# Retention attention into an MLP on one core: y of chunks 2 to 5 for four batches in one block instead of two pairs

## The chip, the cores and the metric

One core of a Trainium2 chip runs the whole kernel. The time is that of the device for one execution, in microseconds; of several runs the median is given. All operands of the matrix products are 16-bit floats (f16), accumulated in 32 bits (f32).

## The reference

Four batches, eight heads, 768 time steps, head size 64. A recurrence with a decay per head gives y, which then goes through an MLP with a tanh-approximated GELU.

```
gamma = 1.0 - 2.0 ** (-5.0 - np.arange(H))
for t in range(S):
    state = gamma * state + einsum('bhd,bhe->bhde', k[:, :, t], v[:, :, t])
    y[:, :, t] = scale * einsum('bhd,bhde->bhe', q[:, :, t], state)
x = y.transpose(0, 2, 1, 3).reshape(B * S, H * D)      # 3072 x 512
h = x @ w_in                                           # 512 -> 2048
out = gelu_tanh(h) @ w_out                             # 2048 -> 512
```

## The kernel before, in words

**Chunks.** Time is cut into six chunks of 128 steps (c = 0 to 5). Within a chunk and a batch b the recurrence becomes matrix products. A = k·q of the chunk (`mm_A`, L272), masked to the causal part on VectorE (`ev_A`, L285, which writes `a_sb`); y = state·q (`mm_yc`, L294) plus v·A (`mm_yi`, L307), accumulated in one PSUM bank and copied to `xT` (`ev_Y`, L231 on ScalarE, L233 on VectorE); S = k·v (`mm_s`, L326), added on VectorE to the decayed state (`ev_S`, L343); the decay for the next chunk on GpSimd (`decay`, L352). A batch takes 8 small matmuls for A (two heads at a time, on the two halves of the array's rows), 4 for `mm_yc` (the whole array), 8 for `mm_yi` (the two halves of its columns), 4 for S (the whole array).

**q and k.** They arrive by DMA from SyncE's queue (`load`), are scaled to f16 on GpSimd (`prep`: L206 for q and kT, L195 for k, L192 for v; for q and kT of chunks 3 to 5, and q of chunk 2), and are transposed per batch by `att_T`: on VectorE (L258), and for k of chunk 2 on TensorE (`mm_T`, L249) with a copy out of PSUM on VectorE (L233). `mm_A` reads the result, `qkT`.

**MLP.** `moe1` (L419) makes 128 hidden features of a chunk for all four batches with 4 matmuls, and ScalarE does the GELU (L434); `moe2` (L452) multiplies back, batch by batch, 16 matmuls each, and `ev_O` copies out (L474 on ScalarE, L472 on VectorE for batch 3) and issues the store from GpSimd's queue (L479).

**Order.** There is no planner for the schedule: instructions go to each engine in the order in which the program emits them. `run(units, after)` emits a list of MLP units, and behind unit i whatever `after[i]` lists. For the loop at L664 the units of chunk c are 16 of `moe1` (0 to 15), then four of `moe2` for each of the four batches (16 to 31), 4 matmuls each; between them the attention of chunk n = c+1 is woven. Chunk 2 (n = 2) is woven into the two runs at L633 and L651: 16 units of `moe1_two` of chunk 1 (8 matmuls of 256 columns each), then 16 units of `moe2` of chunk 1. Each engine is in order, so an instruction that waits holds those behind it.

**`att_AY`** (L369) takes a list of batches `bs` whose y is made and a list `abs_` whose A is made. It emits `mm_yc` of `bs`, `mm_A` of `abs_`, `mm_yi` of `bs`, then the evictions. In chunks 3 to 5 it is called behind unit 12 (A of batches 0 and 1), 18 (y of 0, 1 and A of 2, 3) and 25 (y of 2, 3).

**PSUM.** Eight banks: "h" 2, "o" 2, "att" 4, each handed out in rotation. A of two batches takes all four att banks (`mm_A` takes two for a batch, one for each half of the rows); S and the transposes on TensorE take one att bank each. y of a pair took the two h banks, which `moe1` uses before and after.

Of the kernel before, what the change touches and what calls it, by code (L numbers as in the profile page):

```python
# [16 lines left out]
def kernel(  # L17
# [10 lines left out]
    B, H, S, Dh = q.shape  # L28
# [29 lines left out]
    att = ctx.enter_context(tc.tile_pool(name="att", bufs=4))  # L58
# [170 lines left out]
    def copy_on(eng, out, in_):  # L229
        if eng is nc.scalar:  # L230
            eng.copy(out=out, in_=in_)  # L231
        else:
            eng.tensor_copy(out=out, in_=in_)  # L233
# [5 lines left out]
    def bank(tag, dt=F32, shape=(128, NHP, 128), name="ps"):  # L239
        return psum.tile(list(shape), dt, tag=tag, bufs=BANKS[tag], name=name)  # L240
# [26 lines left out]
    def mm_A(c, b):  # L267
        t = qkT[c, b]
        ps = [bank("att", name=f"a_ps{j}") for j in range(2)]
        for hp in range(NHP):  # L270
            for j in range(2):
                nc.tensor.matmul(  # L272
                    out=ps[j][:, hp],
                    lhsT=t[j * 64:(j + 1) * 64, 1, hp],
                    rhs=t[j * 64:(j + 1) * 64, 0, hp],
                    start=True,
                    stop=True,
                )
        pss["A", c, b] = ps

    def ev_A(c, b):
        ps = pss.pop(("A", c, b))
        for j in range(2):
            s = att.tile([128, NHP, 128], F16, tag=f"a{j}", name=f"a_sb{j}")
            nc.vector.tensor_tensor(out=s, in0=ps[j], in1=mask[:, j], op=ALU.mult)  # L285
            a_sb[c, b, j] = s

    def mm_yc(c, b, tag):
        y_ps = pss["Y", c, b] = bank(tag, name="y_ps")
        if c == 0:  # L290
            return

        for hp in range(NHP):
            nc.tensor.matmul(  # L294
                out=y_ps[:, hp],
                lhsT=st[:, hp, b],
                rhs=qkT[c, b][:, 0, hp],
                start=(hp == 0),
                stop=False,
                skip_group_check=True,  # L300
            )

    def mm_yi(c, b):
        y_ps = pss["Y", c, b]
        for hp in range(NHP):
            for j in range(2):
                nc.tensor.matmul(  # L307
                    out=y_ps[j * 64:(j + 1) * 64, hp],
                    lhsT=h16["v", c, b][:, 2 * hp + j],
                    rhs=a_sb[c, b, j][:, hp],  # L310
                    start=(c == 0),
                    stop=True,
                    skip_group_check=True,
                )

    def ev_Y(c, b, eng=nc.vector):
        if c not in xT:
            xT[c] = xp.tile([128, NHP, B * C], F16, tag="x", name="xT")
        copy_on(eng, xT[c][:, :, b * C:(b + 1) * C], pss.pop(("Y", c, b)))
# [30 lines left out]
    def decay(c, b):  # L350
        if c + 2 < NCk:
            nc.gpsimd.tensor_tensor(  # L352
                out=stg[:, :, b],
                in0=st[:, :, b],
                in1=cst[:, OG:OG + NHP].unsqueeze(2).broadcast_to([128, NHP, 128]),
                op=ALU.mult,
            )
# [6 lines left out]
    def att_S(c, b, tag="att"):  # L364
        mm_s(c, b, tag)
        ev_S(c, b)
        decay(c, b)

    def att_AY(c, bs, tag, ca, abs_, eng):  # L369


        for b in bs:
            mm_yc(c, b, tag)
        for b in abs_:
            mm_A(ca, b)
        for b in bs:
            mm_yi(c, b)
        if tag == "o":
            for b in abs_:
                ev_A(ca, b)  # L380
        for b in bs:
            ev_Y(c, b, eng)
        if tag != "o":
            for b in abs_:
                ev_A(ca, b)
# [50 lines left out]
    def moe1(c, fc):  # L436
        h_ps = bank("h", shape=(128, B * C), name="h_ps")
        moe1_mm(c, fc, h_ps, 0, B * C)
        gelu(g_tile(c, fc)[:, fc % 2], h_ps)
# [57 lines left out]
    def run(units, after):  # L497
        for i, u in enumerate(units):
            u()
            for f, *args in after.get(i, ()):  # L500
                f(*args)

    VE, AC, PO, SY = nc.vector, nc.scalar, nc.gpsimd, nc.sync
# [85 lines left out]
    def units2(c, b, n=4, tag="o"):  # L589
        u = [(lambda i=i: moe2(c, b, range(i, i + n), tag)) for i in range(0, NF, n)]  # L590
        last = u[-1]
        u[-1] = lambda: (last(), ev_O(c, b))
        return u
# [9 lines left out]
    for b in range(B - 1):  # L603
# [8 lines left out]
            8: [(preps, 1, 0)],  # L612
            10: [(att_T, 1, 0), (preps, 1, 1)],
            11: [(att_AY, 1, (), "att", 1, (0,), None)],
            12: [(att_T, 1, 1), (preps, 1, 2)],
            13: [(att_AY, 1, (0,), "h", 1, (1,), AC)],
            14: [(att_T, 1, 2), (preps, 1, 3), (att_S, 1, 0)],
            15: [(att_AY, 1, (1,), "h", 1, (2,), AC), (att_T, 1, 3), (att_S, 1, 1)],
        },
    )  # L620
# [9 lines left out]
    for nm in "kqv":  # L630
        for b in range(B):
# [11 lines left out]
            6: [(att_S, 1, 3)],  # L643
            8: [(att_T, 2, 0), (load, 3)],
            10: [(att_T, 2, 1)],
            12: [(att_AY, 1, (), "o", 2, (0, 1), None)],
            14: [(att_T, 2, 2)],
            15: [(att_T, 2, 3)],
        },
    )  # L650
    run(  # L651
        [x for b in range(B) for x in units2(1, b)],
        {
            2: [(att_AY, 2, (0, 1), "h", 2, (2, 3), AC)],
            4: [(att_S, 2, 0)],
            5: [(att_S, 2, 1)],
            8: [(att_AY, 2, (2, 3), "h", 2, (), AC)],
            10: [(att_S, 2, 2)],
            11: [(att_S, 2, 3)],
        },  # L660
    )

# [1 line left out]
    for c in range(2, NCk - 1):  # L664
        n = c + 1
        after = {
            2: [(prep, n, 0)],
            4: [(prep, n, 1)],
            6: [(prep, n, 2), (att_T, n, 0)],
            8: [(prep, n, 3), (att_T, n, 1)],  # L670
            9: [(load, n + 1)] if n + 1 < NCk else [],
            12: [(att_AY, n, (), "att", n, (0, 1), None)],
            13: [(att_T, n, 2)],
            15: [(att_T, n, 3)],
            18: [(att_AY, n, (0, 1), "h", n, (2, 3), VE)],
            20: [(att_S, n, 0)],
            21: [(att_S, n, 1)],
            25: [(att_AY, n, (2, 3), "h", n, (), AC)],
            27: [(att_S, n, 2)],
            28: [(att_S, n, 3)],  # L680
        }
        run(
            [(lambda fc=fc: moe1(c, fc)) for fc in range(NF)]
            + [x for b in range(B) for x in units2(c, b)],
            after,
        )
    c = NCk - 1
# [36 lines left out]
```

## Time and profile before

| | |
|---|---|
| median of 5 runs | 215.22 us (215.04 to 216.4) |
| profiled execution | 216.08 us, of which the span of the core is 214.3 us |
| TensorE (PE) busy | 206.8 us, 96% of the span, at full granted clock |
| VectorE (DVE), ScalarE (ACT), GpSimd (POOL) busy | 85.7, 86.6, 96.9 us |
| MLP matmuls of 512 columns | 16 units of 4 in a chunk; L452 88.1 us and L419 86.3 us busy in all |
| A, mask on DVE (L285) | 48 instructions, 682 ns each |
| chunk 2's attention ends and chunk 2's MLP begins | 87.14 us |
| MLP of chunks 3, 4, 5 begins | 119.28, 151.43, 182.51 us |

The engines' names in the profile are those in brackets; PEld is TensorE's weight load. In the chain of work each line has a start, a duration from one start to the next, and the engine with the tensor that it writes. In the timeline each line has a start, the busy time, the engine and line of the program, the operation, and in square brackets the idle time before it with what ended it. Matmuls overlap in the pipe, so a single matmul's duration (379 ns for 512 columns) is longer than its spacing (216 ns); the chain gives spacings.

### The profile page before, as it was taken

The page shows a single profiled execution, that of the slowest core. Times are in us where ns is not written, and L with a number is a line of the kernel's source. Part 1 is how long each engine was busy: PE and PEld are TensorE (multiplying, and loading weights), DVE is VectorE, ACT ScalarE, POOL GpSimd, SP SyncE. Part 2 cuts the span into 40 slices and gives each one's busy share as a digit, 9 for nine tenths or more (in the row PEclk, how much of TensorE's full clock was granted, in tenths as well). Part 3 has the DMA queues.
Part 4 walks back from the last instruction along what each step waited for, and adds up shares of the span by engine and source line. Part 5 has one row for each costly group of instructions (what it writes and reads, how often), then busy time and mean ns, then how long its engine had stood idle before and what let it go on. Part 6 is the DMA issues. An engine that isn't in the chain of part 4 may idle for free.

```text
span 214.3 us, 3906 instructions
## 1 busy us (share of the span) xinstructions
PE 206.8 (96%) x1535; PEld 111.9 (52%) x1535; DVE 85.7 (40%) x156; ACT 86.6 (40%) x149; POOL 96.9 (45%) x117
## 2 busy tenths in 40 slices
PE   7899999999998999999999999999999999999992
PEld 2468444467896554444545444545444554444461
DVE  5468000299529443235673335673335640100000
ACT  2467670335464313465113465113465113565110
POOL 2898100253828463699353799221599221100000
PEclk9999999999999999999999999999999999999999
DMA  6999999999879788998878987889900012100121
GB/s 154 288 238 206 206 202 227 235 245 200 164 185 234 111 164 161 238 256 135 126 150 185 284 179 114 125 164 246 284 11 3 0 70 80 49 0 0 52 98 50
DMA packets 124802, 32.79 MB, mean 153 GB/s; under 512 B 118064, under 2 KB 122928, under 8 KB 124784
## 3 DMA queue, kind: packets, MB, share of 16 engines
q1 hardware_dynamic: 106800, 20.22, 48.3%
q0 software_dynamic: 6112, 8.65, 17.3%
q10 hardware_dynamic: 11872, 3.67, 7.3%
q8 instruction: 12, 0.20, 0.4%
q14 instruction: 6, 0.05, 0.1%
HBM read 30.44 MB, written 6.29 MB: 171 GB/s over the span
## 4 chain that ended last, share of the span: by engine, by line
PE 75%; DMA 16%; POOL 4%; DVE 2%; SPq 1%; issue 0%; ACT 0%; DVEq 0%
PE o_ps L452 34%; PE h_ps L419 31%; DMA w_out<-in_moe_w_out_dram 9%; DMA k<-in_k_dram 3%; PE y_ps L307 3%; DMA q<-in_q_dram 3%; PE a_ps L272 3%; PE y_ps L294 2%; PE s_ps L326 2%; DMA out_dram<-o_sb 2%; POOL w_in L400 1%; PE qkT_ps L249 1%; POOL k L195 1%; DVE qkT L258 1%; POOL w_out L409 1%; SPq L98 0%
## 5 line engine op out<-in xcount | busy, mean ns | idle before, releaser
L452 PE MATMUL o_ps<-w_out,g 128*128 128x512 f16 (+1 forms) x400 | 88.1, 371 | 0.0
L419 PE MATMUL h_ps<-xT,w_in 128*128 128x512 f16 (+2 forms) x480 | 86.3, 337 | 0.0
L434 ACT ACTIVATE g<-h_ps 128x512 f16<-128x512 f32 (+1 forms) x98 | 57.7, 589 | 49.3 <-PE h_ps L419 49.1
L419 PEld LDWEIGHTS <-w_in 128*128 128x128 f16 x480 | 44.6, 98 | 37.1
L452 PEld LDWEIGHTS <-g 128*128 128x128 f16 x400 | 37.6, 98 | 38.9
L285 DVE TENSOR_TENSOR a_sb<-a_ps,mask 128x512 f16<-128x512 f32 x48 | 30.1, 682 | 16.2 <-PE a_ps L272 16.1
L195 POOL TENSOR_TENSOR k<-k,cst 128x512 f16<-128x512 f32 x24 | 25.3, 1063 | 11.0 <-DMA k<-in_k_dram 11.0
L479 POOL DMA_DIRECT2D out_dram<-o_sb x17 | 9.6, 568 | 45.2 <-ACT o_sb L474 35.6
L474 ACT COPY o_sb<-o_ps 128x512 f32<-128x512 f32 x19 | 11.0, 586 | 40.9 <-PE o_ps L452 37.8
L352 POOL TENSOR_TENSOR stg<-st,cst 128x512 f32<-128x512 f16 x16 | 16.6, 1046 | 10.8 <-DVE st L343 9.9
L343 DVE TENSOR_TENSOR st<-s_ps,stg 64x256 f16<-64x256 f32 x32 | 13.5, 421 | 17.8 <-PE s_ps L326 17.2
L206 POOL TENSOR_TENSOR q<-q,cst 128x512 f16<-128x512 f32 x16 | 16.6, 1046 | 4.7 <-DMA out_dram<-o_sb 4.6
L258 DVE STREAM_TRANSPOSE qkT<-q 128x512 f16<-128x512 f16 x16 | 11.2, 699 | 15.7 <-POOL q L206 15.7
L195 DVE TENSOR_TENSOR q<-q,cst 128x512 f16<-128x512 f32 x8 | 6.7, 836 | 23.0 <-DMA q<-in_q_dram 22.9
L231 ACT CAST xT<-y_ps 128x512 f16<-128x512 f32 x15 | 8.3, 588 | 11.2 <-PE y_ps L307 11.2
L206 POOL TENSOR_TENSOR kT<-kT,cst 128x512 f16<-128x512 f32 x12 | 12.5, 1044 | 0.0
L171 PE MATMUL spin_ps<-zero 128*128 128x512 f16 x31 | 10.2, 479 | 1.3 <-DVE zero L139 1.3
L491 DVE COPY o_sb<-o_ps 128x256 f32<-128x256 f32 x1 | 0.4, 425 | 25.2 <-PE o_ps L452 25.2
L192 POOL CAST v<-v 128x512 f16<-128x512 f32 x16 | 9.7, 606 | 0.8 <-DMA v<-in_v_dram 0.8
L272 PE MATMUL a_ps<-qkT 64*128 64x128 f16 x192 | 8.3, 218 | 1.5 <-DVE qkT L233 0.8
L190 ACT CAST v<-v 128x512 f16<-128x512 f32 x7 | 4.3, 621 | 12.2 <-DMA k<-in_k_dram 8.7
L258 DVE STREAM_TRANSPOSE qkT<-kT 128x512 f16<-128x512 f16 x12 | 8.3, 691 | 1.8 <-POOL kT L206 1.8
(36 smaller groups left out, 95.7 us busy)
## 6 DMA issues: line engine op xcount, KB each, us to landing
v<-in_v_dram SPq DMA_DIRECT2D x20, 256.0 KB, 4.6
k<-in_k_dram SPq DMA_DIRECT2D x19, 256.0 KB, 5.0
out_dram<-o_sb POOLq DMA_DIRECT2D x17, 256.0 KB, 3.4
q<-in_q_dram SPq DMA_DIRECT2D x64, 64.0 KB, 2.8
kT<-in_k_dram SPq DMA_DIRECT2D x48, 64.0 KB, 3.1
w_out<-in_moe_w_out_dram POOLq DMA_DIRECT2D x4, 512.0 KB, 17.8
q<-in_q_dram SPq DMA_DIRECT2D x6, 256.0 KB, 6.0
w_in<-in_moe_w_in_dram POOLq DMA_DIRECT2D x3, 512.0 KB, 11.6
```

Source lines behind the costliest of these rows:

```text
L171: nc.tensor.matmul(out=ps, lhsT=zero[:, 0:128], rhs=zero, start=True, stop=True)
L195: eng.tensor_tensor(out=t, in0=src, in1=cst[:, col:col + H].unsqueeze(2).broadcast_to([128, H, Dh]), op=ALU.mult,)
L206: nc.gpsimd.tensor_tensor(out=t, in0=ld_all((key, c))[:, b * NHP:(b + 1) * NHP].rearrange("p hp a d -> p (hp a) d"), in1=cst[:, col:col + ...
L258: nc.vector.transpose(out=t[:, i].rearrange("p hp t -> p (hp t)"), in_=blk16.pop((nm, c, b)).rearrange("p ha d -> p (ha d)"),)
L272: nc.tensor.matmul(out=ps[j][:, hp], lhsT=t[j * 64:(j + 1) * 64, 1, hp], rhs=t[j * 64:(j + 1) * 64, 0, hp], start=True, stop=True,)
L285: nc.vector.tensor_tensor(out=s, in0=ps[j], in1=mask[:, j], op=ALU.mult)
L343: eng.tensor_tensor(out=st[sl, :, b, sl], in0=s_ps[sl, :, sl], in1=stg[sl, :, b, sl], op=ALU.add,)
L352: nc.gpsimd.tensor_tensor(out=stg[:, :, b], in0=st[:, :, b], in1=cst[:, OG:OG + NHP].unsqueeze(2).broadcast_to([128, NHP, 128]), op=ALU.mult,)
L419: nc.tensor.matmul(out=out, lhsT=w_in_sb[wi][:, kc, wr * 128:(wr + 1) * 128], rhs=xT[c][:, kc, t0:t1], start=(kc == 0), stop=(kc == NHP - ...
L434: nc.scalar.activation(out=out, in_=in_, func=AF.Gelu_apprx_tanh, scale=1.0)
L452: nc.tensor.matmul(out=ps[:, n0:n1], lhsT=g_sb[c, fc // 2][:, fc % 2, b * C:(b + 1) * C], rhs=w_out_sb[fc // (NF // NO)][:, fc % (NF // NO ...
L474: nc.scalar.copy(out=o_sb, in_=ps)
```

## The change

A new function `att_Y` makes y of all four batches together: `mm_yc` of the four, into the two h banks (batches 0, 1) and two att banks (2, 3), then `mm_yi` of the four, then the evictions, in turn on ScalarE and VectorE. The pairs of A are made by calls of `att_AY` without y. In chunk 2 A of batches 0 and 1 moves from behind unit 12 to behind unit 13 of `moe1_two`, with the transposes of batch 2 directly behind it; A of batches 2, 3 stands behind unit 1 of `moe2`, y behind unit 4 and the four S behind 6 to 9. In chunks 3 to 5 `att_T` of batch 2 stands before A of batches 0, 1, that of batch 3 one unit earlier, A of batches 2, 3 behind unit 17, y behind unit 21 and the four S behind 23 to 26.

```diff
+    def att_Y(c):
+
+        tags = ("h", "h", "att", "att")
+        for b in range(B):
+            mm_yc(c, b, tags[b])
+        for b in range(B):
+            mm_yi(c, b)
+        for b in range(B):
+            ev_Y(c, b, (AC, VE)[b % 2])
...
             10: [(att_T, 2, 1)],
-            12: [(att_AY, 1, (), "o", 2, (0, 1), None)],
-            14: [(att_T, 2, 2)],
+            13: [(att_AY, 2, (), "att", 2, (0, 1), None), (att_T, 2, 2)],
             15: [(att_T, 2, 3)],
...
-            2: [(att_AY, 2, (0, 1), "h", 2, (2, 3), AC)],
-            4: [(att_S, 2, 0)],
-            5: [(att_S, 2, 1)],
-            8: [(att_AY, 2, (2, 3), "h", 2, (), AC)],
-            10: [(att_S, 2, 2)],
-            11: [(att_S, 2, 3)],
+            1: [(att_AY, 2, (), "att", 2, (2, 3), None)],
+            4: [(att_Y, 2)],
+            6: [(att_S, 2, 0)],
+            7: [(att_S, 2, 1)],
+            8: [(att_S, 2, 2)],
+            9: [(att_S, 2, 3)],
...
+            10: [(att_T, n, 2)],
             12: [(att_AY, n, (), "att", n, (0, 1), None)],
-            13: [(att_T, n, 2)],
-            15: [(att_T, n, 3)],
-            18: [(att_AY, n, (0, 1), "h", n, (2, 3), VE)],
-            20: [(att_S, n, 0)],
-            21: [(att_S, n, 1)],
-            25: [(att_AY, n, (2, 3), "h", n, (), AC)],
-            27: [(att_S, n, 2)],
-            28: [(att_S, n, 3)],
+            14: [(att_T, n, 3)],
+            17: [(att_AY, n, (), "att", n, (2, 3), None)],
+            21: [(att_Y, n)],
+            23: [(att_S, n, 0)],
+            24: [(att_S, n, 1)],
+            25: [(att_S, n, 2)],
+            26: [(att_S, n, 3)],
```

## Prediction

> **What bounds the kernel now.** I read the page's chain that ended last first. TensorE carries it, with the MLP's two matmul lines on top:
>
> ```profile
> PE 75%; DMA 16%; POOL 4%; DVE 2%; SPq 1%; issue 0%; ACT 0%; DVEq 0%
> ```
>
> The DMA share lies in the start, before 41 us, which the change doesn't touch. From there to the end TensorE is the path, so the change is worth what it does to TensorE's own stream: its busy time, and its waits. Next the waits of TensorE, and of its weight loads, from 60 to 190 us. In this stretch there are only two places, the second seen at the weight loads:
>
> ```profile
> PE a_ps L272 <- DVE qkT L233: 0.8, 2, 0.5
> ```
> ```profile
> PEld L326 <- DVE a_sb L285: 1.0, 2, 0.5
> ```
>
> The chain in order of time shows what they cost. Chunk 2 first, where A is woven into the first MLP half of chunk 1:
>
> ```profile
> 62.83 1.06 POOL q L206
> 63.89 0.02 issue
> 63.91 0.72 DVE qkT L258
> 64.64 0.02 issue
> 64.66 0.42 DVE qkT L233
> 65.08 0.56 DVE qkT L258
> 65.64 0.38 DVE qkT L233
> 66.02 0.05 issue
> 66.07 0.40 PE a_ps L272 x8
> 66.47 1.85 PE h_ps L419 x16
> ```
>
> For a stretch TensorE isn't the path here: q of chunk 2 lands, GpSimd scales it at 62.83, VectorE transposes two batches one after the other, and A of batch 1 starts at 66.07. The timeline says when TensorE was ready: its 16 matmuls of units 11 and 12 start at 62.96 and take 1.74, so it was free at 64.70. A of two batches takes 0.55 where nothing waits (below), so 66.47 - 64.70 - 0.55 = 1.2 us are lost.
>
> Then chunk 3, the same view; chunks 4 and 5 have the same numbers within 0.02:
>
> ```profile
> 98.36 0.55 PE a_ps L272 x16
> 98.91 2.70 PE h_ps L419 x12
> 101.61 2.59 PE o_ps L452 x12
> 104.20 0.45 PE y_ps L294 x8
> 104.65 0.55 PE a_ps L272 x16
> 105.20 0.57 PE y_ps L307 x16
> 105.77 1.83 PE o_ps L452 x8
> 107.60 0.00 issue
> 107.60 0.40 PE s_ps L326 x4
> ```
>
> Two things. S takes 0.40 where it takes 0.22 everywhere else: 0.18 of waiting for the first att bank that the mask of A (L285) gives back. And each change between whole-array and half-array matmuls costs: twelve MLP matmuls take 2.59, but 2.70 behind A; eight take 1.73 (2 x 0.863), but 1.83 behind y. L307 takes 0.34 for 8 (chunk 1, at 56.77) and 0.57 for 16, so 0.11 of a block is fixed and each further batch costs 0.23; A is the same (0.33, 0.55). L294 has no such part (0.22, 0.45).
>
> **The change part by part.** *Matmuls.* None is added or removed: A, y and S have the same counts. What changes is the number of passages between array shapes. Before, per chunk: into A, out; into A (behind L294), from A into L307, out; into L307, out: seven, 0.11 each. After: into A, out, into A, out, into L307, out: six. Worked out: two A 1.10, out of each 0.22, L294 for four 0.90, L307 for four 0.57 + 2 x 0.23 = 1.03, out 0.10: 3.35. Before: 0.55 + 0.11 + 0.45 + 0.55 + 0.57 + 0.10 + 0.45 + 0.57 + 0.10 = 3.45. A gain of 0.10 to 0.11 in each of four chunks: 0.44. The Trainium skill (TensorEngine Tiling, Key Properties) says that changing the tiling mode drains the engine; the rows price it. By rule and rows the gain is 0.44; if the fixed part belonged to the pair of batches, it would be nothing.
>
> *The wait of S, chunks 3 and 4.* S now stands two units (1.73 us) behind y; its att banks are those of A of batch 3, masked long before, and those of y of batches 2 and 3, copied out in 0.6 us on each of two engines. Gone: 2 x 0.18 = 0.36. What is late next there is nothing: the h banks of y are needed again only by the next chunk's first unit, eight units later.
>
> *Chunk 2, first half.* A moves behind unit 13. TensorE does that unit from 64.70 to 65.57 in the time that it now waits. A of batch 0 runs at 65.57 (its qkT is there at 65.08), A of batch 1 still at 66.07, to 66.40. Then the added wait: the transposes of batch 2 stand directly behind, and need an att bank, all four of which A holds. The mask of the first starts 0.4 us behind A (98.36 to 98.72 in chunk 3), at 65.98, takes 0.68, and the release reaches TensorE 0.06 later (107.54 to 107.60 at S): 66.72, a wait of 0.3. Queued behind it are units 14 and 15 and all of `moe2`; ScalarE's GELU waits for those, with nothing late. Then 0.22 + 1.74 + 0.22: `moe2` starts at 68.90, against 69.64 in the chain. Gain 0.74. Bounds: if the unprofiled runs get q 0.8 earlier, the old wait was only 0.4 and the new bank wait eats the gain (-0.1); without the bank wait it would be 1.1.
>
> *Chunk 2, second half.* VectorE's four masks and two transposes with copies take 4.31 from their start (65.93 to 70.24 before); from 65.98 qkT of batch 3 is ready at 70.29. A of batches 2, 3 stands at 68.90 + 1.73 = 70.63: no wait, by 0.3 and 0.3 more for batch 3. Masks end at 73.5; y starts at 73.9 and needs the last mask 1.5 later. The four S cost 0.22 each as before. Only the 0.11 changes: chunk 2's MLP starts at 69.64 - 0.74 + 17.50 - 0.11 = 86.29, against 87.14.
>
> *Chunk 3, the transposes.* Batch 2's go ahead of the masks of A(0, 1) on VectorE and wait there for GpSimd. GpSimd doesn't move with TensorE: k of batch 0 lands at 91.2 and it works without a gap from there (the profile's only wait is there).
>
> ```profile
> 97.36 1.05 POOL L206 TENSOR_TENSOR kT<-kT,cst 128x512 f16<-128x512 f32 x1
> ...
> 100.93 1.05 POOL L206 TENSOR_TENSOR kT<-kT,cst 128x512 f16<-128x512 f32 x1
> ```
>
> So VectorE transposes kT of batch 2 at 98.44, the masks run from 99.05 to 101.5 (before 98.72), kT of batch 3 from 102.05 to 102.76. TensorE, 0.85 earlier than before, does A(0, 1) at 97.51, then 0.55 + 0.11 + 2.59 + 1.73: A of batch 2 at 102.49, of batch 3 at 102.82. It just fits: the cover is zero, and any further delay of GpSimd is paid one to one. I take 0 (bounds -0.3 to 0.6). In chunks 4 and 5 GpSimd begins behind the store of batch 3's output and so moves with TensorE: in the clock of before kT of batch 3 is transposed at 134.4, and A(3) would stand at 130.51 + 0.66 + 2.59 + 1.73 + 0.33 = 135.8; 1.4 to spare. The stores on GpSimd's queue keep their order against the preps; the loads on SP keep theirs, and none waits for a moved instruction.
>
> *Evictions.* y goes half to ScalarE, half to VectorE in every chunk. They have 0.6 us spacing, and the next reader of `xT` is ten units off. The same page's section PSUM Bottleneck speaks against the change here: packing speeds up TensorE but not the emptying of PSUM, and two more banks are held. By the rows the emptying is 4 x 0.6 over two engines, 1.2 us, against 1.73 until S wants a bank: nothing; without that cover the third S would wait.
>
> **Sum.** 0.74 + 4 x 0.11 + 2 x 0.18 = 1.54. The profiled execution is 216.08 with a span of 214.3: it gives 214.54 and a span of 212.8. The median is 215.22, 0.86 below the profiled one; by the same step 213.7.
>
> **The rivals.**
> *Little is left (215.22 to 214.2).* The 1.2 us of chunk 2 hang on when q lands. If it lands earlier in unprofiled runs, or if chunk 3 takes the gain back because GpSimd's k lands when it lands and A(3) waits, the 0.74 goes: 215.22 - 0.80 = 214.4. For it: the cover of 0 in chunk 3 and the 0.86 between profile and median. Against it: the chain shows the DMA far ahead of chunk 2 and the loads' order on SP unchanged.
> *Slower.* VectorE is in order, and the transposes of batch 2 now stand in front of the masks of A(0, 1). If GpSimd is late by L, VectorE stands, the att banks stay taken, and A(2, 3), one unit and a y block earlier than before, stops TensorE in chunks 3, 4 and 5. Price: L in chunk 3, L - 1.4 in each of the others. From L = 1.45 it eats the 1.54, from 1.8 the kernel is slower by over 0.5%; at L = 2: 2 + 2 x 0.6 - 1.54 = 1.7 more, 216.9. For it: GpSimd has no pause from 91 to 103 and no slack in chunk 3. Against it: it keeps the same queue, and in chunks 4 and 5 waited for no load.
>
> **Chances.** The forecast 58%, little left 27%, slower 10%, better than forecast (no bank wait, 213.2 or below) 5%. Within 0.5% (1.08 us, about what a measurement of this kernel can tell from no change) is from 214.1 to 216.3; a small part of the second case lies below that. Faster 0.63, same 0.27, slower 0.10. Range 213.0 to 215.1: it takes in the second case, and leaves out the slower one and half of the better.
>
> **What would show it.** In the chain after: `moe2` of chunk 1 starting near 68.9, with a wait of L249 for L285 of some 0.3 and none of note at A; L307 x32 at 1.03; S at 0.22 everywhere; MLP of chunk 3 starting near 118.1. I am wrong if A in chunk 3 waits for L258 by more than 0.3, if L307 of four takes 1.14, or if S or y wait for a bank.

## The result, and the profile after

Median 215.19 us (42 runs) against 215.75 us (77 runs of the kernel before). The ratio is 0.9977, with a 95% interval of 0.9967 to 0.9987: 0.3 to 0.7 us less. The prediction said 213.7, 1.5 us less than its median: the sign was right and the size three times too large.

The profiled execution took 215.64 us, with a span of 213.9. First the waits of TensorE from 55 us on in the profile of the change (who waited for whom: total us, times, longest). Two were forecast at chunk 2, none at chunk 3:

```profile
PE a_ps L272 <- DVE qkT L233: 0.4, 1, 0.4
PE a_ps L272 <- DVE qkT L258: 0.3, 1, 0.3
PE qkT_ps L249 <- DVE a_sb L285: 0.2, 1, 0.2
```

The second line is in chunk 3. The chain of the same profile (start, duration, what) shows the place:

```profile
95.88 0.85 POOL k L195
...
98.44 1.02 POOL kT L206
99.46 0.02 issue
99.48 0.04 DVE qkT L258
...
100.12 2.45 DVE a_sb L285 x4
102.56 0.52 DVE qkT L258
103.08 0.02 issue
103.10 0.68 DVE qkT L258
103.78 0.05 issue
103.83 0.40 PE a_ps L272 x8
104.23 3.56 PE o_ps L462 x16
107.78 0.89 PE y_ps L294 x16
108.68 1.01 PE y_ps L307 x32
109.69 1.83 PE o_ps L462 x8
111.53 0.22 PE s_ps L326 x4
```

The reader is to see two things. Up to 103.8 the chain no longer runs through TensorE but through GpSimd and VectorE, and from there back through SyncE's loads: kT of batch 2 is scaled late, the masks of A(0, 1) stand behind its transpose on VectorE (99.48), and the transposes of batch 3 stand behind the masks. What TensorE had saved before that point is gone: chunk 3's MLP begins at 119.33 in the chain, where it was 119.28. Behind it the sums of the prediction hold: S at 0.22, four y at 0.89 and 1.01. The rest is thus as forecast: the MLP of chunk 3 to that of chunk 4 takes 31.85 (32.15 before), and that of chunk 4 to chunk 5 takes 30.96 (31.08 before).

Where that delay begins is a load. GpSimd's timeline of the change, at the first k of chunk 3:

```profile
89.66 1.05 POOL L206 TENSOR_TENSOR kT<-kT,cst 128x512 f16<-128x512 f32 x1
92.27 1.04 POOL L195 TENSOR_TENSOR k<-k,cst 128x512 f16<-128x512 f32 x1 [1.57 <-PE h_ps L429]
```

The releaser named in brackets is not the one that counted. That instruction waits for k's load and for a matmul that was long done, and the chain follows it back to the load: issued on SyncE's queue at 87.30, 4.84 us, to 92.14. The same instruction in the profile before:

```profile
91.23 1.04 POOL L195 TENSOR_TENSOR k<-k,cst 128x512 f16<-128x512 f32 x1 [0.35 <-DMA k<-in_k_dram]
```

There the load was issued at 87.26, at nearly the same time. The scaling began 3.97 us after the issue, and 4.97 in the profile of the change: it is the landing that came 1.0 later.

### The profile page after: what moved, and what is told of

Its sections match the earlier page's. It is cut to its first block, busy times and chain, and to the rows that moved or that the text cites. A ratio compares the mean times of both kernels' runs of the same rounds, so it can differ in the third digit from the quotient of the medians.

```text
span 213.9 us, 3916 instructions
## 1 busy us (share of the span) xinstructions
PE 206.3 (96%) x1535; PEld 111.9 (52%) x1535; DVE 88.4 (41%) x158; ACT 85.4 (40%) x147; POOL 96.7 (45%) x117
## 4 chain that ended last, share of the span: by engine, by line
PE 50%; DMA 19%; SPq 13%; POOL 7%; DVE 6%; issue 3%; ACT 0%; DVEq 0%; POOLq 0%
PE o_ps L462 25%; PE h_ps L429 19%; SPq L110 12%; DMA w_out<-in_moe_w_out_dram 9%; DMA k<-in_k_dram 5%; DMA q<-in_q_dram 3%; DVE a_sb L285 2%; POOL k L195 2%; DMA out_dram<-o_sb 2%; PE y_ps L307 2%; PE a_ps L272 1%; POOL w_in L410 1%; PE y_ps L294 1%; POOL q L206 1%; DVE qkT L258 1%
## 5 line engine op out<-in xcount | busy, mean ns | idle before, releaser
L195 DVE TENSOR_TENSOR q<-q,cst 128x512 f16<-128x512 f32 x8 | 7.2, 902 | 22.6 <-DMA q<-in_q_dram 22.6
L233 DVE CAST xT<-y_ps 128x512 f16<-128x512 f32 x11 | 7.2, 686 | 11.4 <-PE y_ps L307 11.4
L231 ACT CAST xT<-y_ps 128x512 f16<-128x512 f32 x13 | 7.2, 587 | 9.3 <-PE y_ps L307 9.3
L482 DVE COPY o_sb<-o_ps 128x512 f32<-128x512 f32 x4 | 2.8, 691 | 19.0 <-PE o_ps L462 14.7
```

The lines of the kernel that those rows point to most:

```text
L195: eng.tensor_tensor(out=t, in0=src, in1=cst[:, col:col + H].unsqueeze(2).broadcast_to([128, H, Dh]), op=ALU.mult,)
```

## The experiments

Two theories stood against each other. S, supply: up to A of batch 3 in chunk 3 the pace is set by the loads on SyncE's queue and GpSimd's in-order scaling, and what TensorE saves ahead of that point turns into a wait there. K, chance: that wait belongs to one profile, and chunk 2's gain is missing because q comes early enough in most executions. All runs were timed in five rounds beside the kernel before on the same chip, in three sets with a chip each (e1 to e4, e5 to e8, e9 to e12), so across sets the ratios are compared and not the times; each profile is one execution. "Chunk 3 takes" means the stretch from the start of chunk 2's MLP to that of chunk 3's, into which chunk 3's attention is woven.

**e1: the new order in chunk 2 alone.** The loop for chunks 3 to 5 is the old one.

```diff
-            17: [(att_AY, n, (), "att", n, (2, 3), None)],
-            21: [(att_Y, n)],
+            18: [(att_AY, n, (0, 1), "h", n, (2, 3), VE)],
+            25: [(att_AY, n, (2, 3), "h", n, (), AC)],
...
```

> Chunk 2 in the new order, chunks 3 to 5 in the old one. Theory S (the loads on SyncE's queue and GpSimd's prep set the pace up to A of batch 3 in chunk 3): the old order of chunk 3 asks for those transposes about 1 us later, so nothing is taken back there, and the run keeps whatever chunk 2 gained: 0.1 us (second half alone) to 0.85 us (with the 0.74 of the first half) less than before. Theory K (chunk 2 never had a wait worth 0.74 in most executions, q simply lands earlier): 0.1 us or nothing.

Measured: ratio 0.9983 (0.9971 to 0.9995), 0.1 to 0.6 us less. The profile's chunk 3 takes 32.15, as before: nothing is taken back there. The gain is below the 0.85 of the forecast; between the theories it doesn't decide.

**e2: the new order in chunks 3 to 5 alone.**

```diff
-            13: [(att_AY, 2, (), "att", 2, (0, 1), None), (att_T, 2, 2)],
+            12: [(att_AY, 1, (), "o", 2, (0, 1), None)],
+            14: [(att_T, 2, 2)],
...
```

> Chunk 2 in the old order, chunks 3 to 5 in the new one. Theory S: chunks 4 and 5 bring 0.41 us, chunk 3 its 0.29 minus what A of batch 3 waits for the transposes (0.3 to 0.6 us, since TensorE comes there nearly as early as in the full change): 0.1 to 0.4 us less than before, close to the full change. Theory K (the wait in chunk 3 is an accident of one profile): 0.7 us less.

Measured: 0.9963 (0.9946 to 0.9980), 0.8 us less in the middle, nearer to K's number than to S's. In the profile chunk 3 takes 31.85 without a wait of any size at A: k of batch 0 was scaled 4.15 us after the MLP's start in that execution (90.85 to 86.70), and 5.47 us after it in the profile of the change. So the wait is there in some executions and not in others. S needs that addition: it depends on when the load lands against TensorE.

**e3: A of batches 2 and 3 one unit later, in chunk 3 only.**

```diff
-            17: [(att_AY, n, (), "att", n, (2, 3), None)],
-            21: [(att_Y, n)],
+            17 + (n == 3): [(att_AY, n, (), "att", n, (2, 3), None)],
+            21 + (n == 3): [(att_Y, n)],
...
```

> The full change, but in chunk 3 A of batches 2 and 3 and all behind it stand one unit (0.86 us) later. Theory S: the wait of A of batch 3 for VectorE's transposes (0.5 us in the profile of the change) falls to nearly nothing, 0.4 to 0.5 us less than the full change, 0.9 to 1.0 less than before. Theory K: no more than 0.1 us from the full change.

Measured: 214.38 us, 0.9947 (0.9926 to 0.9967), 1.1 us less than before, 0.4 to 0.65 less than the full change (e5 below, and the first result). In its profile k was scaled later against TensorE than in that of the change (5.86 us after the MLP's start), and A still took 0.58 at its new place, against 0.55 where nothing waits. The order alone, with no instruction more or less, brings what S said, in the middle values: the interval overlaps with that of e5 and meets that of the first result, so these times alone don't part the two kernels.

**e4: q and kT of all batches scaled before k and v.** In chunks 3 to 5, on GpSimd.

```diff
             8: [(prep, n, 3), (att_T, n, 1)],
-            9: [(load, n + 1)] if n + 1 < NCk else [],
+            9: [(prep_kv, n, b) for b in range(B)] + ([(load, n + 1)] if n + 1 < NCk else []),
```

(`prep` then holds only q and kT, `prep_kv` the k and v.)

> The full change, but GpSimd scales q and kT of all four batches first and k and v of all four behind them, in chunks 3 to 5. Theory S: kT of batch 3 in chunk 3 is ready some 6 us sooner, because 4 k and 4 v steps (1.05 and 0.6 us each) and the wait for k's load no longer stand ahead of it; the wait of A goes, the masks of A(0,1) no longer queue behind a transpose: 0.5 us less than the full change. If it gives less than e3, the new prep order costs something itself (v comes later). Theory K: no more than 0.1 us from the full change.

Measured: 214.56 us, 0.9951 (0.9929 to 0.9973), 1.06 us less than before. No wait of TensorE's matmuls in chunk 3; A of batches 2 and 3 starts at 102.37 and takes the full 16 matmuls without a break. kT of batch 3 is scaled at 94.93, 4.7 us sooner than in e5 below (99.64) and not 6, since three k and three v stood ahead of it, not four.

**e5: the full change again**, unaltered.

> The full change once more, beside the other kernels of this set. Its time against before should be again about 0.5 us less (0.3 to 0.7). In its profile theory S expects A of batch 3 in chunk 3 to wait for the transpose, by 0.1 to 0.6 us depending on when k's first load of chunk 3 lands; and chunk 2's bank wait to be about 0.6 us where A of both batches runs without waiting, 0.2 where q is late.

Measured: 215.03 us, 0.9965 (0.9947 to 0.9984). Its 22 executions lie from 214.03 to 216.07, those of e3 and e4 from 214.13 to 214.90. The profiled one took 214.43, with a span of 212.7; the prediction's sum was a span of 212.8. Its chain in chunk 3:

```profile
97.51 0.55 PE a_ps L272 x16
98.07 2.70 PE h_ps L429 x12
100.76 1.73 PE o_ps L462 x8
102.49 0.55 PE a_ps L272 x16
103.04 3.56 PE o_ps L462 x16
```

A of batches 0 and 1 at 97.51 and of 2 and 3 at 102.49 are the predicted times to the hundredth, but that is luck, as the table below shows. The wait of A of batch 3 that was expected here, 0.1 to 0.6, is missing. GpSimd's timeline of this execution has k without any wait:

```profile
88.94 1.05 POOL L206 TENSOR_TENSOR kT<-kT,cst 128x512 f16<-128x512 f32 x1
89.94 1.04 POOL L195 TENSOR_TENSOR k<-k,cst 128x512 f16<-128x512 f32 x1
```

Here that load was issued at 85.80, 1.5 us sooner than in the other two profiles. Stretch by stretch, from the timelines:

| us | before | the change | e5 |
|---|---|---|---|
| start to the transposes of batch 1 (the second L249) | 62.74 | 62.86 | 62.44 |
| from there to `moe2` of chunk 1 | 6.73 | 6.56 | 6.31 |
| to the MLP of chunk 2 | 17.50 | 17.38 | 17.38 |
| to the MLP of chunk 3 | 32.15 | 32.36 | 31.85 |
| to the MLP of chunk 4 | 32.15 | 31.86 | 31.85 |
| to the MLP of chunk 5 | 31.08 | 30.96 | 30.96 |

The first row lies ahead of every instruction that the change moves, and yet it runs from 62.03 to 62.93 over all fourteen profiles. So 0.30 of e5's distance from the profile before is not the change's. Behind it e5 saves 1.26, and the profile of the change, where the loads were late, 0.49. The predicted places came out because 0.30 at the start and 0.42 in the second row stand by chance for the 0.74 that was forecast in the second row alone.

**e6: k of chunk 3 loaded late.** The dose.

```diff
-            for nm in "vk":
-                load1(nc.sync, nm, c, b)
+        order = "vk" if c != 3 else "vvvvkkkk"
...
```

> The full change, but of chunk 3's loads the four v go before the four k on SyncE's queue, so that k of batch 0 is issued some 3 us later while q, kT and all else keep their places. Theory S: GpSimd stands at k of batch 0, kT of batch 3 is scaled some 2 to 3 us later, and A of batch 3 in chunk 3 waits that much: 1.5 to 3 us more than the full change, slower than before. Theory K, or any cause in chunk 2: within 0.2 us of the full change.

Measured: 218.43 us, 1.0140 (1.0098 to 1.0181), 3.4 us more than e5 in the median; its three executions at full granted clock took 217.88 to 218.19, about 2.9 more. GpSimd starts that k at 95.23, and the waits of TensorE in its profile are

```profile
PE a_ps L272 <- DVE qkT L258: 3.5, 2, 2.0
PE a_ps L272 <- DVE qkT L233: 0.5, 1, 0.5
PE qkT_ps L249 <- DVE a_sb L285: 0.2, 1, 0.2
```

The first line grew from 0.3 to 3.5 in total, in chunk 3, by one permutation of eight loads: once at A of batch 1 (1.48), once at A of batch 3 (1.99). The first of the two places hadn't been reckoned with. Chunk 3 takes 37.32 in this profile, 5.5 more than in e5, and the waits at A are only 3.5 of that. Most of the rest is TensorE's clock. The page's row of the granted clock, and in the chain the MLP block behind A, which takes 3.56 elsewhere:

```profile
PEclk9999999999999999999889999999999999999999
107.17 5.21 PE o_ps L462 x16
```

From 107.5 to 110.0 the granted clock was 0.50; that block lost 1.65 by it. The other two executions above 218.2 had a mean granted clock of 0.990 and 0.996, so the clock may account for the part of the 3.4 above the expected 3; what brought it down isn't shown. As an account of chunk 3 K is refuted all the same: at full clock too, a later k ends the kernel later by 2.9. What K said of chunk 2 is another matter, and held in part (below).

**e7: q of chunk 2 loaded earlier.**

```diff
-    for b in range(B):
+    for b in range(2):
         load1(SY, "k", 2, b)
     load_blk("q", 2)
+    for b in range(2, B):
+        load1(SY, "k", 2, b)
...
```

(GpSimd scales in that order: k of 0, 1, q of 0, 1, then k, q of 2 and of 3, then v.)

> The full change, but on SyncE's queue q of chunk 2 is loaded before k of batches 2 and 3 and not behind them, and GpSimd scales in that order. q lands some 2 to 3 us earlier. Chunk 2's A then never waits for q; the bank wait of 0.6 us behind it stays, so chunk 2 is at its best already in the executions in which q is in time: 0.0 to 0.3 us less than the full change in chunk 2. Theory S: TensorE only comes earlier to chunk 3 and waits there, so nothing of it, 0.0 to 0.1, is left at the end.

Measured: 0.9976 (0.9957 to 0.9995), no difference from the full change. q is scaled from 60.03, 1.4 to 3.4 us sooner than in the profiles with the old loading order, and A of both batches runs at once; but the bank wait stands at 0.56 (the profile names GpSimd's v as its releaser, but the stretch to `moe2` is 6.30, that of e5) and chunk 3 still waits (it takes 32.25).

**e8: e4 and e7 together.**

> e4 and e7 together: q of chunk 2 loaded earlier, and q and kT of all batches scaled first in chunks 3 to 5. Theory S: no wait for transposes in chunk 3, so what e7 gains in chunk 2 stays: 0.0 to 0.3 us less than e4, 0.5 to 0.8 less than the full change. Theory K: as the full change.

Measured: 214.32 us, 0.9937 (0.9917 to 0.9956), 1.4 us less than before. Against e4 it is 0.3 us less, within what the two intervals leave open. Against e7, timed beside it and apart from it by nothing but e4's order of scaling, it is 0.8 us less (0.9937 against 0.9976), and the intervals don't meet. That is the clearest timed evidence that the late scaling in chunk 3 costs the changed kernel time. The two profiles show 0.40 of it (32.25 and 31.85); the rest isn't located.

**e9: e4 without the bank wait.**

```diff
-            13: [(att_AY, 2, (), "att", 2, (0, 1), None), (att_T, 2, 2)],
+            13: [(att_AY, 2, (), "att", 2, (0, 1), None)],
+            14: [(att_T, 2, 2)],
```

> e4, but the transposes of batch 2 in chunk 2 stand behind unit 14 and not directly behind A of batches 0 and 1, so that the mask has 0.87 us to give a bank back. Theory S, with the bank wait of 0.56 seen in the profiles as a real cost: L249's wait is gone and moe2 of chunk 1 starts 0.5 us sooner after the transposes of batch 1 (5.8 in place of 6.3); 0.4 to 0.5 us less than e4. If the bank wait only hides another wait (A of batches 2 and 3 in chunk 2 then waiting for its transposes): 0 to 0.2.

Measured: 213.92 us, 0.9934 (0.9910 to 0.9957), 0.4 us less than e4 in the middle, with intervals that overlap; the cost is shown by the profiles. TensorE's timeline of chunk 2, first in e5 (with the wait in brackets), then in e9:

```profile
62.44 0.39 PE L249 MATMUL qkT_ps<-iden,k 128*128 128x128 f16 x4
65.38 0.62 PE L272 MATMUL a_ps<-qkT 64*128 64x128 f16 x16
66.56 0.38 PE L249 MATMUL qkT_ps<-iden,k 128*128 128x128 f16 x4 [0.56 <-DVE a_sb L285]
68.53 0.39 PE L249 MATMUL qkT_ps<-iden,k 128*128 128x128 f16 x4
68.75 1.89 PE L462 MATMUL o_ps<-w_out,g 128*128 128x512 f16 x8
```
```profile
62.05 0.39 PE L251 MATMUL qkT_ps<-iden,k 128*128 128x128 f16 x4
64.98 0.62 PE L274 MATMUL a_ps<-qkT 64*128 64x128 f16 x16
66.42 0.39 PE L251 MATMUL qkT_ps<-iden,k 128*128 128x128 f16 x4
67.52 0.39 PE L251 MATMUL qkT_ps<-iden,k 128*128 128x128 f16 x4
67.74 1.89 PE L464 MATMUL o_ps<-w_out,g 128*128 128x512 f16 x8
```

From the transposes of batch 1 to `moe2` 6.31 in e5, 5.69 in e9: the bank wait cost 0.6.

**e10: all three edits** (e8 with that of e9).

> e8 (q of chunk 2 loaded earlier, q and kT scaled first) with the transposes of batch 2 as in e9. The version to which the theory points: no wait of TensorE for attention from chunk 2 on. 0.4 to 0.5 us less than e8: about 1.8 us less than before (ratio 0.992).

Measured: 213.81 us, 0.9929 (0.9904 to 0.9953), 1.5 us less than before: faster than the kernel before and than the change in its first set (0.9967 to 0.9987), with an interval that just overlaps with e5's, and in the middle a little short of the expected 0.992. Its profile has no wait of TensorE's matmuls from 45 to 190 us. Against e8 the profile saves the same 0.6, of which the timed runs show 0.2, within their intervals.

**e11: e4 with y made in pairs** inside `att_Y`.

```diff
-        for b in range(B):
-            mm_yc(c, b, tags[b])
-        for b in range(B):
-            mm_yi(c, b)
+        for bs in ((0, 1), (2, 3)):
+            for b in bs:
+                mm_yc(c, b, tags[b])
+            for b in bs:
+                mm_yi(c, b)
```

> e4, but att_Y makes L294 and L307 of batches 0 and 1 and then of 2 and 3 (same matmuls, banks and evictions). That is one passage out of the half-array shape and one into it more, in each of four chunks. If a passage costs the 0.10 to 0.11 that the prediction reads from the rows: 0.21 a chunk, 0.8 us more than e4. If the fixed part belongs to the first block behind an MLP unit and not to the shape: nothing.

Measured: 1.0002 (0.9985 to 1.0019) against e4's 0.9951, 1.1 us more in the middle. The chain in chunk 3:

```profile
106.42 0.45 PE y_ps L296 x8
106.86 0.57 PE y_ps L309 x16
107.43 0.55 PE y_ps L296 x8
107.98 0.57 PE y_ps L309 x16
```

The second L296 takes 0.55 where the first takes 0.45 (the passage out), and the two L309 take 1.14 where 32 in one block take 1.01 (the passage in): 0.23 a chunk, 0.9 in four. The price of a passage is shown.

**e12: the kernel before with e4's order of scaling.**

> The kernel before, with q and kT of all batches scaled before k and v in chunks 3 to 5, as in e4. Theory S: the old order asks for the last transposes of chunk 3 about 1 us later and had no wait there, so this alone gives nothing: within 0.2 us of before. If the prep order is a gain by itself (masks no longer delayed on VectorE, S no longer waiting), 0.3 us or more, and then e4 says less about the wait in chunk 3.

Measured: 0.9986 (0.9970 to 1.0001), 0.3 us less in the middle and not told apart from none. The same edit gave 0.3 to 0.6 us on top of the full change in the middle values of e5 and the first result, and 0.8 on top of e7. By the times alone a part of that could be a gain that the edit brings to any order. The profiles show none: chunks 3 to 5 take 32.14, 32.15 and 31.08 here, as before, while with the new order e4 has 31.85 in chunk 3 for 32.36. Whether the kernel before also waits in chunk 3 in some executions, no profile shows.

Not run was the kernel before with e7's earlier q alone. By the table in the next section its stretch in chunk 2 would fall from about 6.50 toward the 5.69 of e9: up to 0.8 us, an estimate, without y in one block.

## Why the prediction was wrong in size

By its own steps:

- *Matmuls, 0.44: right.* L307 of four batches was put at 1.03 and takes 1.01, L294 at 0.90 and takes 0.89. Chunk 5, which has nothing else, lost 0.12. e11 gives the price back.
- *The wait of S, 0.36: right.* S takes 0.22 everywhere; chunk 4 lost 0.30 in all, 0.29 was predicted.
- *Chunk 2, second half, 0.11: right.* From the start of `moe2` to chunk 2's MLP 17.38 in the timeline of e5 and of the profile of the change, 17.50 before.
- *Chunk 2, first half, 0.74: mis-sized, by three terms.* In all, the old order lost 1.04 there (6.73 less the 5.69 of e9, where nothing waits) and not 1.2, and the new order loses 0.6 of it again. First, the sum took a start from the timeline (68.90) away from one of the chain (69.64). The chain counts a piece from the end of the one before, and the timeline has that same point at 69.47: 0.17 never existed. Second, the bank comes free 0.15 later than forecast: A starts 0.11 after its unit's end, with the passage in front of it, and L249 follows 1.18 behind A's start (65.38 to 66.56 in e5), not 1.15. Where A of both batches runs through, it ends sooner, and the wait is 0.56 and not 0.3. Third, and most: the old wait of 1.2 us was read from one execution. The table has the stretch from the transposes of batch 1 (the second L249) to `moe2`, and how much later than that start GpSimd begins to scale q.

| order in chunk 2 | q after the transposes | stretch |
|---|---|---|
| old: before, e2, e12 | 0.09, -0.02, -0.47 | 6.73, 6.62, 6.17 |
| new: after, e6 | 0.54, 0.69 | 6.56, 6.71 |
| new: e3, e4, e11, e1, e5 | -0.14, -0.09, -0.48, -0.65, -1.04 | 6.31, 6.30, 6.31, 6.31, 6.31 |

The old order follows q one to one; the new one has a floor of 6.31, set by the bank. At the q of the profile before, the gain is 0.42 (0.74 - 0.17 - 0.15); at that of e12 it is a loss of 0.14. Over the eleven profiles that have this loading order (the ten in the table and e9, at -0.26) q's median is -0.14, where the old order takes about 6.50: a gain of 0.2 in place of 0.74. Eleven executions are few, so this 0.2 is an estimate; e1's 0.1 to 0.6 for all of chunk 2 agrees with it.
- *Chunk 3, "It just fits: the cover is zero ... I take 0": this step failed.* That load's landing against TensorE differs between executions (k is scaled 3.81 us after the MLP's start in e5, 4.15 in e2, 5.36 in e7, 5.47 in the profile of the change). Chunk 3 takes 31.85, 31.85, 32.25 and 32.36: by the last two, what exceeds 4.96 is paid one to one, as the prediction said. The bound of 0.6 that the prediction kept for it was right for the profile; but with a cover of zero a spread to one side only costs, and zero was the best case, not the middle. e3 and e4, which give that cover back, are 0.3 to 0.65 us below the two sets of the full change in the middle, and e8 is 0.8 below e7.

Corrected: 0.2 + 0.11 + 0.29 + 0.29 + 0.11 = 1.0 without the wait of chunk 3, where e3 and e4 have 1.1; less a wait of 0.3 to 0.6 on the average, 0.4 to 0.7, where the change has 0.5 and 0.75. The average wait is itself taken from these timed runs, so the last step is a consistency and no test; the profiles show waits of 0, 0.40 and 0.51 (e5, e7, the change). The mechanism that won is the first rival, given 27%: both of its halves held, q that lands earlier in most executions and chunk 3 that takes the gain back because k lands when it lands. The path in chunk 3, masks behind a transpose that waits for GpSimd, is that of the second rival, but at 0.4 to 0.5 and in chunk 3 alone. That the profiled execution lay 0.86 above the median was in hand as a sign that its span (1.7 to 1.8 below the time in the profiles before, after and e5) held something that most executions don't, and it was carried along as if it were fixed. Against the medians of the profiles, 0.32 of it lies ahead of the second L249 (62.74 for 62.42) and 0.23 in the late q (6.73 for 6.50); the rest isn't located.

## What to carry to other kernels

When a change lets the bound engine run ahead, follow it to the next place where it meets work that doesn't move with it, here loads on a queue and an in-order helper, and treat a cover of zero there as a cost, not as a fit. The wait that one profile shows next to a DMA is one draw; before it goes into a sum at full size, see how the runs spread and where the profiled one stands among them. And behind a block that holds every bank of a pool, leave a unit of other work before the next that wants one; where the helper's queue mixes what is needed first with what is needed later, sort it: with three such edits, none of which removes an instruction, the change brought 1.5 us (e10) where alone it brought 0.5 to 0.75. Before two single profiles are compared, compare a stretch that the change can't have touched; here it differed by up to 0.9 us.

## What was not expected of the hardware

Eight loads in another order, v before k, made the kernel 2.9 us slower than e5 at full clock, and 3.4 in the median, with the same bytes (e6), because one instruction on GpSimd stood for 4.93 us ahead of the scaling of q and kT of three batches, whose loads had been issued before it. In the profiled execution TensorE's granted clock then stood at 0.50 from 107.5 to 110.0, right behind the second wait; a wait can thus be followed by more time lost than its own length, though that the wait caused it isn't shown.

The executions of the full change spread wider than those of the kernels that give the cover back: over 2.0 us in e5 and 2.2 in e7, over 0.7 to 0.95 in e3, e4 and e8. These have fewer executions (7 to 12 for 22), and the kernel before, without that wait in its profile, spreads as wide (1.7 to 2.65), so the wait isn't shown to be the cause. Half of e5's executions lie at 215.2 or above, and none of those was profiled: what sets them apart stays open.
